# Leftover tokens of a fused attention and SwiGLU kernel: four batches as one seven-product block, with loads, sums and kept results moved

## The chip, the cores and the metric

The kernel runs on one core of one Trainium2 chip. The metric is the device time of one execution in microseconds (us); smaller is better. The profile is one execution recorded by the hardware profiler. In it PE is the matrix engine, PEld its weight loads, DVE the vector engine, ACT the scalar engine, POOL the GpSimd engine and SP the engine that only issues transfers here. SPq, ACTq and POOLq are the instruction queues of those engines where they issue transfers.

## The reference

For each batch and head (8 batches, 8 heads, 576 tokens, 64 per head), `phi` gives weights that squeeze the keys and values into 32 memory rows; the queries attend to these rows; the heads side by side are the input of a gated feed-forward block.

```
a      = softmax(phi, axis=tokens)                 # (b, h, 576, 32)
k_m    = a^T k ;  v_m = a^T v                      # (b, h, 32, 64)
attn   = softmax(q k_m^T / 8)                      # over the 32 rows
x      = heads side by side of attn v_m            # 4608 tokens x 512
g, val = x @ w_gate, x @ w_val                     # 512 x 1536 each
out    = (g * sigmoid(g) * val) @ w_out            # 1536 x 512, float32
```

## The kernel before

The work goes batch by batch. The kernel multiplies `v_m` into the gate and value weights first (`u_round`, L459, giving U), so that x is never formed: gate and value of a batch come straight from the attention weights A (`t_A`) and U. This is done in 24 slots of four matrix products of 288 tokens (`gv_slot`, L544: gate on PE, SiLU on ACT at L531, value on PE, product with the gate on DVE at L537 into `t_h`). The hidden 1536 rows are held as three chunks c of 512. Slots 0 to 7 make chunk 0, 8 to 15 chunk 1, 16 to 23 chunk 2.

The output product of a batch covers 512 of its 576 tokens by Strassen's scheme in Winograd's form (`products`, L676): seven half-size products instead of eight. Each is 12 matrix instructions (three chunks, two row blocks, two token blocks of 128, each 128x256). Sums of the hidden tokens (`t_S`) are made in `chunk_done` (L585): on POOL for chunks 0 and 1, on DVE for chunk 2, four operations of 128x512 each. Weight sums (`t_T`) are made once. The products use three PSUM banks, "s", "a" and "c"; a bank is added to over several products, so a partial result has to be copied aside first (`keep`, L727: p1, q6 and p5 by ACT). DVE adds the kept parts to the banks for c11, c22 and c12 (`add`, L733), and c21 is a copy. The results lie in the tiles o1 and o2 and go out through `store` (L635).

The 64 last tokens of each batch do not fit that scheme. `chunk_done` copies them into `t_x` (L591), which holds a pair of batches, so 128 tokens; `out_rest` (L643) multiplies them in the ordinary way: per pair and half of the columns 12 matrix instructions of 128x256, one copy and two stores. One such half is run in each of the stages of batches 2 to 7, and the last two halves at the end.

The order is written by hand. The loop at L954 runs for batches 2 to 7; one pass is called a stage here. A stage of batch b goes:

- first product of batch b-1, scores of b (`scores`, L396), part of U, and the rest of 36 "units" of b-1's products (a unit is two matrix instructions), among which DVE makes the inverse sums and the normed weights (`z_inv_v`, `norm`), and ACT makes exp(phi) of batch b+1 (`phi_exp`, L174, instruction L176);
- then the 24 slots. Beside slot 8 PE sums keys and values of batch b+1 (`kv_items`, L297), the denominators coming from a tree of sums on POOL (`phi_sum`, L209, tiles `t_es` and `t_ehl`), and at slot 19 to 20 it makes most of U of batch b+1 (`u_three`, L793). The remaining units are laid between the slots (`spread`, L804), some by `take` beside these two.

`spread` gives items fractional slot positions and sorts them. What an engine does is thus the order in which this program emits it; each engine runs its own instructions in that order. POOL also issues the loads of q, phi, k and v (`loads`, L940, four transfers for batch b+2); for b above 2 they are issued at the head of the stage (L984), for b = 2 at slot 7 to 8 (L1021). SP issues stores and the two transposing transfers (`load_qT` L118, `kv_T` L283). At the end, after `box["end"]` is set, stores alternate between SP and ACT (L637).

After the loop come the seven products of batch 7 and the two halves of `out_rest` of the last pair (L1030 to L1038).

Of the kernel before, what the change touches and what calls it, by code (L numbers as in the profile page):

```python
# [14 lines left out]
def kernel(  # L15
# [569 lines left out]
    def chunk_done(b, c):  # L585

        if b % 2 == 0 and c == 0:
            xs[b // 2] = hpool.tile([128, NJF, 2, 64], BF16, tag="xs", name="t_x")

        def ends():  # L590
            nc.gpsimd.tensor_copy(  # L591
                out=xs[b // 2][:, 4 * c:4 * c + 4, b % 2], in_=hts[b, c][:, :, S - 64:S]
            )

        t = upool.tile([128, 4, 2, 256], BF16, tag=f"U{c}" if b == 1 else f"S{c}", name="t_S")
        Ss[b, c] = t
        A11, A12, A21, A22 = blocks(b, c)

        def sums(eng, part=(0, 1, 2, 3)):
            if 0 in part:  # L600
                eng.tensor_tensor(out=t[:, 0], in0=A21, in1=A22, op=ALU.add)  # L601
            terms = ((t[:, 0], A11), (A11, A21), (A12, t[:, 1]))
            for n in part:
                if n:
                    subtract(eng, t[:, n], *terms[n - 1])

        end = c + 1 == NCH
        if (b, c) in ((0, 2), (1, 1), (1, 2)):
            late.append(lambda *part: sums(nc.gpsimd if b else nc.vector, *part))
        else:  # L610
            sums(nc.vector if end else nc.gpsimd)
        if end and b > 1:
            late.append(ends)
        else:
            ends()
        if (b, c) in beside_sums:
            beside_sums[b, c]()

    beside_sums = {
        (0, 0): lambda: (load_phi(3, nc.gpsimd), load_q_group(2, 0)),  # L620
        (1, 0): lambda: (load_q_group(2, 1), load_q(3)),
        (0, 1): lambda: (load_k(3), load_v(3)),
    }

    def token_segments(b, t0, count):
        segs = []
        t = t0
        while t < t0 + count:
            blk, pp = divmod(t, P)
            n = min(P - pp, t0 + count - t)  # L630
            segs.append((t - t0, n, b, 2 * (blk % 3) + blk // 3, pp))
            t += n
        return segs

    def store(t_o, b, t0, count, row=0, cols=slice(0, 512), queues=None):  # L635

        if queues is None and box.get("end"):  # L637
            queues = nc.sync, nc.scalar
        for n, (r0, m, bb, jj, pp) in enumerate(token_segments(b, t0, count)):
            eng = queues[n % len(queues)] if queues else nc.sync  # L640
            eng.dma_start(out=out_r[bb, jj, pp:pp + m, cols], in_=t_o[row + r0:row + r0 + m])

    def out_rest(pair, half):  # L643

        h = DM // 2
        mine = {}
        cols = slice(h * half, h * half + h)

        def unit(n):
            def run():  # L650
                if n == 0:
                    mine["p"] = bank([128, h], FP32, "p_oo")
                for jf in (2 * n, 2 * n + 1):
                    nc.tensor.matmul(  # L654
                        mine["p"],
                        lhsT=xs[pair][:, jf].rearrange("p a t -> p (a t)"),
                        rhs=WO[jf][:, cols],
                        start=(jf == 0),
                        stop=(jf == NJF - 1),
                    )  # L660
                if n == NJF // 2 - 1:
                    t_o = work.tile([128, h], FP32, tag="to", name="t_o")
                    copy("v" if box.get("end") else "a", t_o, mine["p"])
                    done(mine["p"])
                    end = 2 * pair + 2 == B
                    for k in range(2):
                        store(
                            t_o, 2 * pair + k, S - 64, 64, 64 * k, cols,
                            ((nc.sync, nc.scalar)[k],) if end else None,
                        )  # L670

            return run

        return [unit(n) for n in range(NJF // 2)]

    def products(b, by_hand):  # L676

        h = DM // 2
        mine = {}
        lo, hi = slice(0, h), slice(h, DM)  # L680

        def A(e, n):
            return lambda c, m, u: hts[b, c][
                :, 2 * m + e, 256 * n + 128 * u:256 * n + 128 * u + 128
            ]

        def Sx(n):
            return lambda c, m, u: Ss[b, c][:, n, m, 128 * u:128 * u + 128]

        def W_(e, cols):  # L690
# [5 lines left out]
        def product(home, lhs, rhs, after):  # L696
            def unit(k):
                c, m = k // 2, k % 2

                def run():  # L700
                    fresh = k == 0 and home not in mine
                    if fresh:
                        mine[home] = bank([128, 2, h], FP32, f"p_o{home}")
                        mine[home, "new"] = True
                    for u in range(2):
                        nc.tensor.matmul(  # L706
                            mine[home][:, u],
                            lhsT=lhs(c, m, u),
                            rhs=rhs(c, m),
                            start=fresh and u == 0,  # L710
                            stop=(k == 5),
                            skip_group_check=u == 1 or not mine.get((home, "new")),
                        )
                    if k == 5:
                        mine[home, "new"] = False
                        if after in now:
                            now[after]()

                return run

            return [unit(k) for k in range(6)]
# [4 lines left out]

        def keep(name, home):  # L727
            def run():
                nc.scalar.copy(out=tile_of(name, tag=name, bufs=1), in_=mine[home])

            return run

# [3 lines left out]
                done(mine[home])  # L736

        def both(name, t0, cols):
            for u in range(2):
                store(mine[name][:, u, cols], b, t0 + 128 * u, 128, cols=cols)  # L740

        def c11():
            t = tile_of("o1", (128, 2, DM), tag="to")
            add(t[:, :, lo], "a", "p1", True)
            if box.get("end"):
                both("o1", 0, lo)

        def c22():
            t = tile_of("o2", (128, 2, DM), tag="to")
            add(t[:, :, hi], "s", "p5")  # L750
            if box.get("end"):
                both("o2", 256, hi)

        def c12():
            t = mine["o1"]
            add(t[:, :, hi], "c", "q6", True)
            both("o1", 0, hi if box.get("end") else slice(0, DM))

        def c21():
            t = mine["o2"]  # L760
            copy("v" if box.get("end") else "a", t[:, :, lo], mine["s"])
            done(mine["s"])
            both("o2", 256, lo if box.get("end") else slice(0, DM))

        ops = dict(
            p1=keep("p1", "s"), q6=keep("q6", "s"), p5=keep("p5", "c"),
            c11=c11, c22=c22, c12=c12, c21=c21,
        )
        now = {n: f for n, f in ops.items() if n not in by_hand}
        first = product("s", A(0, 0), W_(0, lo), "p1") + product("a", A(1, 0), W_(1, lo), "c11")  # L770
        five = product("c", Sx(0), T(0), "p5")
# [1 line left out]
        three = product("c", Sx(3), W_(1, hi), "c12")  # L773
        seven = product("s", Sx(2), T(2), "c22")
        four = product("s", A(1, 1), T(3), "c21")
        if b + 1 == B:
            return first + six + five + seven + three + four, ops
        return first + five + six + three + seven + four, ops

# [174 lines left out]
    for b in range(2, B):  # L954
# [23 lines left out]
            backlog = one[6:12] + zero[36:] + one[12:36]  # L978
            ops = ops1
        else:  # L980
            backlog += out_rest(b // 2 - 1, b % 2)
            run(take(6))
        if b > 2:
            loads(b)  # L984
        for g in range(NG):
            scores(b, g)
        if b > 2:
# [16 lines left out]
        run(take(12))  # L1004
        if b == 2:
            u_three(2)
            run(out_rest(0, 0))
            u_values(2)
            backlog = one[36:]
        g = gv_slots(b)  # L1010
        beside = 0 if last else min(7, len(backlog))
        outs = [lambda: run(take(1)) for _ in range(len(backlog) - beside)]
        streams = [(g, 0, 24), (outs, 4, 24)]
        if last:
            streams += [([u_item(b, 2)], 5, 6)]
        if not last:
            load_qT(b + 1)
            if b > 2:
                phi_sum(b + 1)
            else:  # L1020
                streams += [([lambda: loads(2)], 7, 8)]  # L1021
            streams += [
                (kv_items(b + 1, lambda: (u_item(b, 2, "aava")(), run(take(2)))), KV, KV + 4),
                ([lambda: (run(take(2)), u_three(b + 1), run(take(3)))], 19, 20),
            ]
        spread(*streams)
        flush_mul()
        units, ops = products(b, ("p1", "c11"))
        backlog += units
    run_late()  # L1030
    run(take(6))
    ops["p1"]()
    run(out_rest(B // 2 - 1, 0))
    box["end"] = True
    run(take(6))
    ops["c11"]()
    run(backlog)
    run(out_rest(B // 2 - 1, 1))  # L1038
# [1 line left out]
_INS = ['q', 'k', 'v', 'phi', 'moe_w_gate', 'moe_w_val', 'moe_w_out']  # L1040
_OUTS = [((4608, 512), 'float32')]
# [25 lines left out]
```

The softmax here doesn't subtract the row's maximum and nothing guards it: scores larger than these inputs give would overflow.

## Time and profile before

| what | value |
|---|---|
| median of 3 runs | 238.11 us (237.35 to 239.08) |
| the profiled execution's own time | 236.3 us |
| its span, first to last instruction | 234.5 us |
| PE busy | 225.9 us (96%) |
| DVE, ACT, POOL busy | 187.4, 172.5, 135.2 us |
| leftover products, L654 | 96 matrix instructions of 128x256 |
| seven-product instructions, L706 | 672 of 128x256 |
| granted clock of PE | 1.000 |
| q, phi, k and v loads, 576 KB each | 7.4, 7.9, 10.1 and 14.4 us median from issue to landing |

Busy time of PE counts an instruction[...], so neighbouring instructions overlap: the mean of 273 ns for a 128x256 instruction isn't what one costs in a row of them. The chain of waits, in which each piece begins where the one before it ends, gives that. The table of busy shares in 40 slices shows in which part of the span an engine works. The table of waits tells for whom an engine stood idle.

### The profile page before, as it was taken

What the parts mean: (1) busy time and instruction counts of PE and PEld (TensorE: products, weight loads), DVE (VectorE), ACT (ScalarE), POOL (GpSimd) and SP (SyncE); (2) the same over time, 40 slices, a digit from 0 to 9 for tenths busy, and PEclk for the clock granted to TensorE, in tenths of its full rate; (3) what the DMA queues carried; (4) which work ended last, traced back from release to release, by engine and by line L of the source; (5) the groups of instructions that cost most, each with busy time, mean ns of one, the idle gap of its engine ahead of it and who ended that gap; (6) DMA issues with size and microseconds to landing.
All of it is one profiled execution on the core that took longest, in us unless ns stands there. A gap on an engine that the chain in (4) does not pass through costs nothing.

```text
span 234.5 us, 7300 instructions
## 1 busy us (share of the span) xinstructions
PE 225.9 (96%) x2847; PEld 171.3 (73%) x2847; DVE 187.4 (80%) x417; ACT 172.5 (74%) x368; POOL 135.2 (58%) x171
## 2 busy tenths in 40 slices
PE   7998899999999999999999999999999999999992
PEld 2555466778887777887778777877788777878881
DVE  4157699999979697998799878988799879987621
ACT  2758888988447888977898779968897789677310
POOL 8532426999099159654992399267916493029400
PEclk9999999999999999999999999999999999999999
DMA  6999999999974999899559964999313721122134
GB/s 211 205 205 207 198 208 206 228 238 248 207 169 97 252 216 158 166 247 232 137 80 252 214 110 106 225 226 142 110 25 81 132 89 27 31 62 89 33 92 126
DMA packets 42914, 36.84 MB, mean 157 GB/s; under 512 B 15488, under 2 KB 38528, under 8 KB 42880
## 3 DMA queue, kind: packets, MB, share of 16 engines
q0 software_dynamic: 21440, 22.42, 55.0%
q1 hardware_dynamic: 20176, 12.79, 25.8%
q10 hardware_dynamic: 1264, 1.18, 1.6%
q8 instruction: 22, 0.36, 0.6%
q14 instruction: 12, 0.10, 0.1%
HBM read 42.47 MB, written 9.44 MB: 221 GB/s over the span
## 4 chain that ended last, share of the span: by engine, by line
PE 82%; DMA 8%; POOL 4%; DVE 3%; issue 1%; ACT 0%; DVEq 0%; POOLq 0%
PE p_g L514 20%; PE p_v L514 19%; PE p_os L706 16%; PE p_oc L706 8%; DMA t_kv<-in_v_dram 8%; PE p_u L471 5%; PE p_oo L654 5%; PE p_oa L706 4%; PE p_kv L235 2%; POOL t_es L217 1%; POOL t_q L108 1%; PE p_g L400 1%; POOL t_kv L98 1%; DVE t_lz L443 1%; DVE t_z L434 1%
## 5 line engine op out<-in xcount | busy, mean ns | idle before, releaser
L537 DVE TENSOR_TENSOR t_h<-t_sg,p_v 128x288 bf16<-128x288 bf16 x192 | 83.1, 452 | 15.6 <-PE p_v L514 7.6
L514 PEld LDWEIGHTS <-t_U 128*128 128x128 bf16 x768 | 73.7, 98 | 21.7 <-issue 2.9
L531 ACT ACTIVATE t_sg<-p_g 128x288 bf16<-128x288 f32 x192 | 74.5, 423 | 15.9 <-PE p_g L514 9.1
L514 PE MATMUL p_g<-t_A,t_U 128*128 128x288 bf16 x384 | 77.2, 286 | 0.0
L514 PE MATMUL p_v<-t_A,t_U 128*128 128x288 bf16 x384 | 77.0, 286 | 0.0
L706 PEld LDWEIGHTS <-t_S 128*128 128x128 bf16 x384 | 37.4, 98 | 4.5 <-issue 0.2
L601 POOL TENSOR_TENSOR t_S<-t_h 128x512 bf16<-128x512 bf16 x17 | 19.7, 1156 | 35.2 <-DVE t_h L537 35.2
L491 ACT CAST t_U<-p_u 128x512 bf16<-128x512 f32 x53 | 28.0, 608 | 8.9 <-PE p_u L471 8.9
L706 PEld LDWEIGHTS <-t_h 128*128 128x128 bf16 x288 | 27.3, 98 | 7.8 <-issue 4.0
L706 PE MATMUL p_os<-t_T,t_S 128*128 128x256 bf16 x192 | 23.7, 273 | 0.0
L559 POOL TENSOR_TENSOR t_S<-t_S,t_h 128x512 bf16<-128x512 bf16 x17 | 19.6, 1155 | 1.3
L559 POOL TENSOR_TENSOR t_S<-t_h,t_S 128x512 bf16<-128x512 bf16 x17 | 20.1, 1186 | 0.0
L559 POOL TENSOR_TENSOR t_S<-t_h 128x512 bf16<-128x512 bf16 x17 | 19.6, 1155 | 0.0
L471 PE MATMUL p_u<-W,t_kT 64*32 64x512 bf16 (+1 forms) x416 | 15.9, 363 | 0.1
L706 PE MATMUL p_os<-t_T,t_h 128*128 128x256 bf16 x96 | 15.6, 273 | 0.0
L827 PE MATMUL p_warm<-bones 128*128 128x512 bf16 (+2 forms) x43 | 12.9, 427 | 1.7 <-DVE bones L850 1.7
L451 DVE TENSOR_TENSOR t_A<-t_E,t_lz 128x576 bf16<-128x576 bf16 x16 | 13.4, 840 | 0.9 <-ACT t_lz L427 0.3
L654 PE MATMUL p_oo<-WO,t_x 128*128 128x256 bf16 x96 | 14.0, 273 | 0.0
L495 DVE CAST t_U<-p_u 128x512 bf16<-128x512 f32 x19 | 12.4, 683 | 1.6 <-PE p_u L471 1.6
L215 POOL COPY t_mark<-t_A 1x1 bf16<-1x1 bf16 x4 | 0.7, 182 | 20.3 <-DVE t_A L451 20.3
L706 PE MATMUL p_oc<-t_T,t_S 128*128 128x256 bf16 x96 | 12.0, 273 | 0.0
L706 PE MATMUL p_oa<-WO,t_h 128*128 128x256 bf16 x96 | 11.8, 273 | 0.0
(93 smaller groups left out, 309.9 us busy)
## 6 DMA issues: line engine op xcount, KB each, us to landing
t_kv<-in_k_dram POOLq DMA_DIRECT2D x8, 576.0 KB, 10.1
t_kv<-in_v_dram POOLq DMA_DIRECT2D x8, 576.0 KB, 14.4
out_dram<-t_o SPq DMA_DIRECT2D x21, 192.0 KB, 2.6
t_phi<-in_phi_dram POOLq DMA_DIRECT2D x6, 576.0 KB, 7.9
t_q<-in_q_dram POOLq DMA_DIRECT2D x5, 576.0 KB, 7.4
out_dram<-t_o SPq DMA_DIRECT2D x37, 64.0 KB, 2.0
out_dram<-t_o SPq DMA_DIRECT2D x14, 128.0 KB, 5.8
t_q<-in_q_dram POOLq DMA_DIRECT2D x6, 288.0 KB, 11.3
```

The lines of the kernel that those rows point to most:

```text
L451: nc.vector.tensor_tensor(out=a, in0=es.pop((b, g)), in1=lzs.pop((b, g)), op=ALU.mult)
L471: nc.tensor.matmul(p[g][32 * i:32 * i + 32, o:o + n], lhsT=kTs[b][64 * g:64 * g + 64, 2, 32 * i:32 * i + 32], rhs=w_part(w, c, i, g, halve ...
L491: nc.scalar.copy(out=t, in_=p)
L495: nc.vector.tensor_copy(out=t, in_=p)
L514: nc.tensor.matmul(p[:, 0:HALF], lhsT=Us[b, c, g][:, o // 2, which, 128 * (o % 2):128 * (o % 2 + 1)], rhs=atts[b, g][:, r], start=(g == 0) ...
L531: nc.scalar.activation(out=sg, in_=gate[:, 0:HALF], func=AF.Silu)
L537: nc.vector.tensor_tensor(out=dst, in0=sg, in1=val[:, 0:HALF], op=ALU.mult)
L559: eng.tensor_tensor(out=out, in0=x, in1=y, op=ALU.subtract)
L601: eng.tensor_tensor(out=t[:, 0], in0=A21, in1=A22, op=ALU.add)
L654: nc.tensor.matmul(mine["p"], lhsT=xs[pair][:, jf].rearrange("p a t -> p (a t)"), rhs=WO[jf][:, cols], start=(jf == 0), stop=(jf == NJF - 1),)
L706: nc.tensor.matmul(mine[home][:, u], lhsT=lhs(c, m, u), rhs=rhs(c, m), start=fresh and u == 0, stop=(k == 5), skip_group_check=u == 1 or n ...
L827: nc.tensor.matmul(p[:, 0:128 * a], lhsT=bones, rhs=x.to_broadcast([128, a, 128]) if a > 1 else bones, start=True, stop=True,)
```

## The change

Four edits:

1. The leftover tokens of four batches (two pairs, 256 tokens) go through the seven-product scheme as well ("quad"), with one token block of 128 instead of two, so 6 matrix instructions to a product. `out_rest` is gone. Quad 0 (batches 0 to 3) is spread over slots 0 to 6 of the stage of batch 4. Of quad 1 (batches 4 to 7) the first two products lie between the slots of the last stage, the other five at the very end. The sums it needs are made by `quad_sums` on POOL, 12 operations of 128x256: for quad 0 in the stage of batch 4, before its scores, and for quad 1 after the last chunk.
2. The loads of batch b+2 are issued in `chunk_done` after the sums of chunk 0, for batch 2 also.
3. The sums of the quads are made in the order in which the products use them, and one term overwrites `t_x`.
4. The results of the quads are put into the second or first half of the tiles p1, q6 and p5 that hold the kept products, and stored from there.

Fewer units are kept back for the `take` calls beside slots 8 and 20 (4 instead of 7), and the stores at the end alternate over a running count.

```diff
             ends()
+        if b > 1 and c == 0:
+            loads(b)
         if (b, c) in beside_sums:
             beside_sums[b, c]()
...
+    def quad_sums(qd):
+        x, y = xs[2 * qd], xs[2 * qd + 1]
...
+        for n in range(4):
+            for c in range(NCH):
+                t = Qs[qd, c]
+                A11, A12, A21, A22 = quarters(c)
+                if n == 0:
+                    nc.gpsimd.tensor_tensor(out=t[:, 0], in0=A21, in1=A22, op=ALU.add)
+                elif n == 1:
+                    subtract(nc.gpsimd, t[:, 1], t[:, 0], A11)
+                elif n == 2:
+                    subtract(nc.gpsimd, A21, A11, A21)
+                else:
+                    subtract(nc.gpsimd, t[:, 2], A12, t[:, 1])
...
-    def out_rest(pair, half):
...
-    def products(b, by_hand):
+    def products(b, by_hand, quad=None):
...
+        U = 2 if quad is None else 1
...
         def keep(name, home):
             def run():
-                nc.scalar.copy(out=tile_of(name, tag=name, bufs=1), in_=mine[home])
+                t = tile_of(name, tag=name, bufs=1)[:, 0:U]
+                mine[name, "all"], mine[name] = mine[name], t
+                nc.scalar.copy(out=t, in_=mine[home])
...
+        def leftover(name, room, half, cols):
+            def run():
+                t = mine[room, "all"][:, half]
...
+        if quad is not None:
+            ops.update(
+                c11=leftover("c11", "p1", 1, lo), c12=leftover("c12", "q6", 1, hi),
+                c22=leftover("c22", "p5", 1, hi), c21=leftover("c21", "q6", 0, lo),
+            )
...
-            backlog += out_rest(b // 2 - 1, b % 2)
             run(take(6))
-        if b > 2:
-            loads(b)
+        if b == 4:
+            run_late()
+            quad_sums(0)
...
-            run(out_rest(0, 0))
+            run(one[36:])
...
-        beside = 0 if last else min(7, len(backlog))
+        quad = []
+        if b == 4:
+            quad = products(b, (), 0)[0]
+        if last:
+            rest, rest_ops = products(b, (), 1)
+            backlog += rest[:12]
+        beside = 0 if last else min(4, len(backlog))
-        streams = [(g, 0, 24), (outs, 4, 24)]
+        streams = [(g, 0, 24), (quad, 0, 6), (outs, 6 if quad else 4, 24)]
...
-                streams += [([lambda: loads(2)], 7, 8)]
...
-                ([lambda: (run(take(2)), u_three(b + 1), run(take(3)))], 19, 20),
+                ([lambda: (u_three(b + 1), run(take(2)))], 19, 20),
...
     run_late()
+    mark = att.tile([1, 1], BF16, tag="mark", bufs=1, name="t_mark")
+    nc.gpsimd.tensor_copy(out=mark, in_=Ss[B - 1, 2][0:1, 3, 0, 0:1])
+    quad_sums(1)
     run(take(6))
     ops["p1"]()
-    run(out_rest(B // 2 - 1, 0))
     box["end"] = True
     run(take(6))
     ops["c11"]()
     run(backlog)
-    run(out_rest(B // 2 - 1, 1))
+    run(rest[12:])
```

## The prediction

> **What bounds the kernel now.** I read the page first: busy shares, and the 40 slices.
>
> ```profile
> PE 225.9 (96%) x2847; PEld 171.3 (73%) x2847; DVE 187.4 (80%) x417; ACT 172.5 (74%) x368; POOL 135.2 (58%) x171
> ...
> PE   7998899999999999999999999999999999999992
> ```
>
> PE is full in every slice from about 30 us to the last one. "Busy" can hide gaps, so the chain of waits is next, here for the end of the span. Its columns are start, duration, engine, tile and line.
>
> ```profile
> 218.37 1.31 PE p_os L706 x12
> 219.68 1.31 PE p_oo L654 x12
> 220.99 1.31 PE p_oa L706 x12
> ...
> 228.85 1.32 PE p_oo L654 x12
> ```
>
> Twelve 128x256 instructions take 1.31 us, whether they belong to a seven-product or to the leftovers: 109 ns each, each piece beginning where the last ended. So PE sets the time, and a PE instruction removed is worth 109 ns where nothing else steps in. One stage, from 118.94 to 144.17 in the chain, is 25.23 us. Its row costs are 96 instructions at 109 ns (10.5), 96 gate and value ones at 122 ns (11.7), scores and first U 0.6, sums of keys and values 0.8, U 1.2: 24.8. Only some 0.4 us of a stage is not PE's own work, about 2 us in five stages.
>
> Then the waits of PE's weight loads (who for whom, us in all, times, longest):
>
> ```profile
> PEld L263 <- POOL t_ehl L224: 0.6, 3, 0.3
> ```
>
> In three of the four stages with this sum (batches 3, 5, 6: 0.32, 0.17 and 0.16 us) PE stands at the denominators until POOL's tree of sums is done. That tree starts when DVE has the normed weights, so here DVE and POOL together already run level with PE.
>
> Last, POOL and ACT in order of time around a stage's turn (batch 3 to batch 4; start, duration, engine, line, instruction):
>
> ```profile
> 109.25 1.15 POOL L601 TENSOR_TENSOR t_S<-t_h 128x512 bf16<-128x512 bf16 x1 [3.25 <-DVE t_h L537]
> ...
> 119.05 0.81 POOL L115 DMA_DIRECT2D t_q<-in_q_dram  x1
> 119.86 0.80 POOL L93 DMA_DIRECT2D t_phi<-in_phi_dram  x1
> ```
>
> ```profile
> 124.08 1.17 ACT L176 ACTIVATE t_ephi<-t_phi 128x1152 bf16<-128x1152 f32 x1
> 125.14 0.58 ACT L729 COPY t_q<-p_os 128x512 f32<-128x512 f32 x1
> ```
>
> The first gives the pace of POOL's sums and the price of issuing loads; the second shows that exp(phi) stands on ACT just ahead of the copy q6 that bank "s" needs before the seventh product.
>
> **What the Trainium skill says.** "TensorE: Matmul & The Clock Gate", section Back-to-back issue gap, gives 262 cycles for 256 columns at 2.4 GHz, 109 ns; the chain agrees (1.31/12). "DMA: Bandwidth & Descriptors", Anatomy of one DMA, says that "any semaphore wait happens on the issuing sequencer before dispatch", so a store issued by ACT that waits for DVE holds up what stands behind it on ACT. At the end of the kernel before, ACT's seven stores fill 4.11 us while it waits for DVE, which fits. "GPSIMD Engine Reference", section 3.1, puts a two-input operation at about 2.6 cycles per element, at 1.2 GHz 1.11 us for 512; the trace has 1.155, so it agrees.
>
> **The change, part by part.**
>
> *PE work.* Out go 8 halves of 12 = 96 instructions; in come 2 quads of 7 x 6 = 84. Minus 12 x 109 ns = **-1.31 us**. Nothing else changes on PE in number. Before the end of the last stage 72 go and 42 + 12 come (-1.96); after it 24 go and 30 come (+0.65).
>
> *Where a filler leaves a wait.* In the order of the changed kernel one unit (two instructions, 0.22 us) that lay between slots 6 and 7 is gone from the stages of batches 3, 5 and 6. It is ahead of the denominators, where PE already waits. The DVE and POOL chain to that point isn't shortened, so the wait grows as much as the work shrinks: 3 x 0.22 = **+0.66**. In batch 4's stage quad 0 stands in front of the denominators (42 x 109 ns = 4.6 us), which hides the rest.
>
> *Sums of the quad on POOL.* No 128x256 bf16 sum is in the trace; bounds are half of 1.155 (0.58) and the float32 row of L217 (0.73). I take 0.60: 12 x 0.60 = 7.2 us. In batch 4's stage POOL then ends: sums of chunk 0 start 8.6 us before the stage's turn (9.69 before the change, less ten instructions), +4.95 with the copy, +3.13 of loads, +4.95 chunk 1, +0.45 copy, +7.2, +4.0 for the tree (127.24 to 131.24 before) = 16.1 us after the turn. PE is at the denominators 12.53 + 4.58 - 0.22 = 16.9 after it. Hidden by 0.8; at 0.73 us a sum it would cost 0.8. Quad 1's sums begin 2.6 us after the last gate product and end at 9.8, before their last use: nothing.
>
> *Loads moved.* Four issues, 0.81 + 0.80 + 0.76 + 0.76 = 3.13 us of POOL, now stand ahead of the sums of chunk 1. Those end about 4.0 us after the turn and are first used 3.75 after it, by the product that needs only the first of them (done at 0.7): nothing. But the data come later against their use. Phi is issued 4.95 + 0.81 = 5.8 us after chunk 0's sums start and lands 7.9 later (four stages: 7.2 to 7.9), so at 13.7. ACT wants it 124.08 - 109.25 = 14.8 less ten instructions (1.09) = 13.7 after the same point. A dead heat. ACT late by d delays q6; q6 ends at 125.72 and the seventh product starts at 126.01 to 126.18, so about 0.3 is free. I take **+0.2** for four stages; bounds 0 and 0.7 each. V, issued at 7.3, lands 13.0 to 13.7 later, at 21 at most, against its use at 20.9; but that row was held up by the transposing transfers, which now run before the loads. Nothing, bounded by 0.5 a stage. The transfer of q into its transposed form, freed of the loads, landed in 6.6 instead of 9.3 to 9.6 us where none ran: no gain, since PE waited 0.2 us for these in all.
>
> *ACT and DVE in the gates.* Each leftover half was one ACT copy (0.41). A quad has three ACT copies, one more copy, three DVE sums (0.42 from the 128x256 row). In quad 0's slots PE has 0.76 us more per slot, which covers them. Elsewhere DVE needs 0.48 us a slot and PE 0.49: fewer fillers take away its catching up. DVE's idle time in those slots was about 2 us, against 1.3 removed: nothing, bounded by 0.4 a stage.
>
> *Result tile p1.* Quad 1's c11 lies in the single buffer p1. Its last product ends 0.73 us before the last gate product, DVE's sum some 0.8 later, SP issues two stores (0.45 each) that land 2.0 after issue: 2.5 us after the turn T. Batch 7's own copy p1, on ACT, needs the buffer and came 1.3 after T. It would end at 3.15, and the third product, which adds to the same bank, is due at 2.62 now that the leftover half no longer lies between. **+0.5** (0.2 to 0.8).
>
> *ACT's queue at the end.* Batch 7's fourth product ends 9.16 after T (84 instructions, without the delay above). DVE's copy takes 0.69 to 9.9, ACT issues two of the four stores, waiting for it: 10.8. Only then comes the quad's q6 copy (0.4), to 11.25. The quad's seventh product, due at 9.16 + 12 x 0.109 = 10.47, adds to that bank: **+0.8** (0.3 to 1.2). Before, an ordinary half lay there, which waits for no copy. The tail (DVE copy 0.42, one store on each queue) is as before.
>
> Sum: -1.31 + 0.66 + 0.2 + 0.5 + 0.8 = **+0.85 us**. The profiled execution would go from a span of 234.5 to 235.4, and from 236.3 to 237.2. The median of the runs lies 1.8 above that execution; the difference is carried over to it: 238.11 + 0.85, **239.0 us**.
>
> **The rivals.**
>
> *The covers hold* (the two waits at the end and the growth at the denominators come to a few tenths): the PE saving remains, 238.11 - 1.31 + 0.3 = 237.1. For it: each wait hangs on differences of under 1 us. Against: buffer p1 and the order on ACT are in the instruction order, and DVE's and POOL's chain isn't shortened.
>
> *Phi comes late* (slower than before). At the turn the loads share the transfer engines with four stores of the batch before. If phi lands 9 us after issue, d is 1.1, PE's seventh product loses 0.8 in each of four stages, +3.2 for 0.2: 242. It decides over the 1% line when phi takes about 8.7 us. Against: at 94.6, with such stores running, it took 7.9. This is also the case in which "a third into the gates" is not what happens: the issue stands behind phi's tree and chunk 0's sums on POOL, nearer the last third.
>
> *DVE becomes the bound in slots without fillers*: 0.4 in batches 3, 5 and 6, +1.2: 240.2. For it: 0.48 against 0.49. Against: DVE's idle 2 us.
>
> **How the numbers follow.** Likeliest case 0.52 (238.3 to 239.8); covers hold 0.22 (236.8 to 238.3); phi late 0.14 (240.3 to 242.5); DVE 0.10 (239.8 to 240.8); something not seen 0.02. A range of 237.1 to 241.0 leaves out the low end of the second and the high half of the third, under 2 in 10. Measurement tells about 1% (2.4 us) from no change. Faster by more than that would need PE's saving and half of all its other time: 0.03. Slower: most of phi late, 0.13. Same: 0.84.
>
> **What would show it.** L654 gone, 84 more at L706's place; the wait at the denominators about 0.4 in batches 3, 5, 6 and none in 4; exp(phi) idle before it, released by its transfer, under 0.5; a gap on PE of about 0.5 before the third product after the last gate, and one of 0.8 before the quad's seventh, with ACT storing. I am wrong if PE's chain has no such gaps (then 237.1), or if ACT waits over 1 us for phi in several stages (then over 241).

## The result and the profile after

| what | before | after |
|---|---|---|
| median of 6 runs | 237.12 us (236.50 to 239.08) | 250.07 us (249.40 to 252.25) |
| ratio | | 1.055, 95% interval 1.049 to 1.061 |
| profiled execution: time, span | 236.3, 234.5 us | 249.44, 247.6 us |

The change makes the kernel 12.9 us slower. The forecast was 239.0 us, with a range of 237.1 to 241.0.

The page of the changed kernel, busy shares and the row of PE in the 40 slices:

```profile
PE 227.4 (92%) x2835; PEld 170.6 (69%) x2835; DVE 198.0 (80%) x423; ACT 172.9 (70%) x368; POOL 154.0 (62%) x196
...
PE   7998999999999999599987999879996999999883
```

PE's 12 instructions are gone (2847 to 2835), as planned, but PE's row, full before, now has holes at slices 17, 21 to 22, 26 to 27 and 31. They are one stage (some 4 to 5 slices of 6.2 us) apart. DVE has 10.6 us more of busy time than before, though only six instructions of 0.42 us have come in.

The table of waits, of PE and of its weight loads (who for whom; us in all, times, longest):

```profile
PE p_g L514 <- DVE t_A L451: 9.6, 4, 2.7
...
PE p_os L715 <- ACT t_q L740: 0.9, 1, 0.9
PE p_os L715 <- ACT t_p L740: 0.8, 1, 0.8
```

```profile
PEld L263 <- POOL t_ehl L224: 1.2, 3, 0.4
```

The first row did not exist before: four times PE stands at the first gate products of a batch, because DVE has not finished the normed weights. The other rows are those that the prediction had: the two gaps of the end, and the denominators (1.2 us, where the kernel before has 0.6).

Where the span grew, in us, measured between the starts of each stage's first product, the "turn" into that stage ("expected" is the kernel before plus what the prediction's steps put into that stage, without the 0.2 for phi):

| part | before | expected | after | after less expected |
|---|---|---|---|---|
| up to the stage of batch 3 | 93.1 | 91.8 | 92.4 | 0.5 |
| stage of batch 3 | 25.6 | 24.5 | 27.5 | 2.9 |
| 4, with quad 0 | 25.2 | 28.5 | 31.4 | 2.9 |
| 5 | 25.3 | 24.2 | 27.0 | 2.7 |
| 6 | 25.3 | 24.2 | 27.0 | 2.8 |
| 7 | 23.6 | 23.6 | 23.8 | 0.2 |
| the end | 16.3 | 18.3 | 18.7 | 0.4 |

So the unexpected loss lies in the stages of batches 3 to 6, 2.7 to 2.9 us in each. PE's four waits for the normed weights are 2.73, 2.40, 2.24 and 2.25 us of it, in this order.

Why DVE is late shows in DVE's own groups. First of the kernel before, then after: the second of the four sums of chunk 2 (us busy in all, mean ns of one, idle before):

```profile
L559 DVE TENSOR_TENSOR t_S<-t_S,t_h 128x512 bf16<-128x512 bf16 x7 | 3.4, 490 | 0.2
```

```profile
L559 DVE TENSOR_TENSOR t_S<-t_S,t_h 128x512 bf16<-128x512 bf16 x7 | 6.5, 934 | 0.2
```

The same instruction, on the same data, takes about twice as long on average; the other three get longer too (442 to 989, 442 to 663 and 462 to 627 ns). What stands beside it is shown by POOL and DVE in order of time at the turn into the stage of batch 4, which is at 119.81 (start, duration, engine, line, instruction):

```profile
118.41 0.75 POOL L102 DMA_DIRECT2D t_kv<-in_v_dram  x1
119.17 1.17 POOL L601 TENSOR_TENSOR t_S<-t_h 128x512 bf16<-128x512 bf16 x1
120.42 1.16 POOL L559 TENSOR_TENSOR t_S<-t_S,t_h 128x512 bf16<-128x512 bf16 x1
121.53 1.34 POOL L559 TENSOR_TENSOR t_S<-t_h 128x512 bf16<-128x512 bf16 x1
122.83 1.33 POOL L559 TENSOR_TENSOR t_S<-t_h,t_S 128x512 bf16<-128x512 bf16 x1
```

```profile
121.13 0.73 DVE L601 TENSOR_TENSOR t_S<-t_h 128x512 bf16<-128x512 bf16 x1
121.89 1.26 DVE L559 TENSOR_TENSOR t_S<-t_S,t_h 128x512 bf16<-128x512 bf16 x1
123.07 1.37 DVE L559 TENSOR_TENSOR t_S<-t_h 128x512 bf16<-128x512 bf16 x1
124.36 0.61 DVE L559 TENSOR_TENSOR t_S<-t_h,t_S 128x512 bf16<-128x512 bf16 x1
...
130.18 1.22 DVE L451 TENSOR_TENSOR t_A<-t_E,t_lz 128x576 bf16<-128x576 bf16 x1
```

The loads end at 119.16, and only then do POOL's sums of chunk 1 begin, 119.17 to 124.16. DVE's sums of chunk 2 fall into the same time. Both engines read two inputs from SBUF, and both get longer. DVE's four sums take 3.77 us from the first start to the start of what follows (121.13 to 124.90), where the kernel before needed 1.65; POOL's last two go from 1.15 to 1.34.

In the kernel before the two rows did not meet. There the turn is at 118.77. POOL's last sum of chunk 1, then DVE's first sum of chunk 2 and the second normed weights:

```profile
117.62 1.16 POOL L559 TENSOR_TENSOR t_S<-t_h,t_S 128x512 bf16<-128x512 bf16 x1
```

```profile
119.65 0.42 DVE L601 TENSOR_TENSOR t_S<-t_h 128x512 bf16<-128x512 bf16 x1
...
126.42 0.76 DVE L451 TENSOR_TENSOR t_A<-t_E,t_lz 128x576 bf16<-128x576 bf16 x1
```

POOL's sums are over at 118.78, and DVE's begin 0.87 us later.

### The profile page after: what moved, and what is told of

Its sections match the earlier page's. It is cut to its first block, busy times and chain, and to the rows that moved or that the text cites. A ratio compares the mean times of both kernels' runs of the same rounds, so it can differ in the third digit from the quotient of the medians.

```text
span 247.6 us, 7309 instructions
## 1 busy us (share of the span) xinstructions
PE 227.4 (92%) x2835; PEld 170.6 (69%) x2835; DVE 198.0 (80%) x423; ACT 172.9 (70%) x368; POOL 154.0 (62%) x196
## 4 chain that ended last, share of the span: by engine, by line
PE 63%; DVE 22%; POOL 4%; issue 4%; ACT 3%; DMA 1%; ACTq 0%; DVEq 0%; SPq 0%; POOLq 0%
PE p_g L514 17%; PE p_v L514 16%; PE p_os L715 11%; DVE t_S L559 5%; PE p_u L471 4%; PE p_warm L862 4%; PE p_oc L715 4%; POOL t_es L217 3%; DVE t_lz L443 3%; DVE t_z L434 3%; DVE t_A L451 2%; DVE t_o L745 2%; DVE t_h L537 2%; PE p_kv L235 2%; PE p_oa L715 2%
## 5 line engine op out<-in xcount | busy, mean ns | idle before, releaser
L537 DVE TENSOR_TENSOR t_h<-t_sg,p_v 128x288 bf16<-128x288 bf16 x192 | 82.0, 452 | 16.9 <-PE p_v L514 5.3
L514 PE MATMUL p_g<-t_A,t_U 128*128 128x288 bf16 x384 | 78.0, 286 | 9.7 <-DVE t_A L451 9.6
L601 POOL TENSOR_TENSOR t_S<-t_h 128x512 bf16<-128x512 bf16 x17 | 19.7, 1160 | 40.3 <-DVE t_h L537 40.2
L559 POOL TENSOR_TENSOR t_S<-t_h,t_S 128x512 bf16<-128x512 bf16 x17 | 20.8, 1228 | 0.0
L559 POOL TENSOR_TENSOR t_S<-t_h 128x512 bf16<-128x512 bf16 x17 | 20.3, 1195 | 0.0
L715 PE MATMUL p_os<-t_T,t_h 128*128 128x256 bf16 x96 | 14.7, 274 | 0.3 <-DVE t_o L745 0.3
L451 DVE TENSOR_TENSOR t_A<-t_E,t_lz 128x576 bf16<-128x576 bf16 x16 | 13.9, 871 | 0.9 <-ACT t_lz L427 0.3
L715 PE MATMUL p_oc<-WO,t_S 128*128 128x256 bf16 x96 | 11.8, 272 | 0.0
L715 PE MATMUL p_os<-WO,t_h 128*128 128x256 bf16 x96 | 11.8, 272 | 0.0
## 6 DMA issues: line engine op xcount, KB each, us to landing
WO<-in_moe_w_out_dram POOLq DMA_DIRECT2D x3, 512.0 KB, 18.7
```

The costliest lines, as they stand in the source:

```text
L451: nc.vector.tensor_tensor(out=a, in0=es.pop((b, g)), in1=lzs.pop((b, g)), op=ALU.mult)
L514: nc.tensor.matmul(p[:, 0:HALF], lhsT=Us[b, c, g][:, o // 2, which, 128 * (o % 2):128 * (o % 2 + 1)], rhs=atts[b, g][:, r], start=(g == 0) ...
L537: nc.vector.tensor_tensor(out=dst, in0=sg, in1=val[:, 0:HALF], op=ALU.mult)
L559: eng.tensor_tensor(out=out, in0=x, in1=y, op=ALU.subtract)
L715: nc.tensor.matmul(mine[home][:, u], lhsT=lhs(c, m, u), rhs=rhs(c, m), start=fresh and u == 0, stop=(k == 5), skip_group_check=u == 1 or n ...
```

## The experiments

Each ratio below is against the kernel before as it was measured beside the run.

The theory: POOL and DVE hinder each other where both run operations with two SBUF inputs. The moved loads cost only because they push POOL's sums of chunk 1 onto DVE's sums of chunk 2. The rivals: the transfers themselves are at fault; or POOL's 12 sums for the quad.

**e1, loads back.** The changed kernel, with the loads where they were before.

```diff
-        if b > 1 and c == 0:
-            loads(b)
...
+        if b > 2:
+            loads(b)
         if b == 4:
             run_late()
             quad_sums(0)
```

> The changed kernel with the loads issued where the kernel before has them (slot 7 to 8 for batch 2, head of the stage for the others), all else as changed. Crowding theory (the moved loads push POOL's sums of chunk 1 into the time of DVE's sums of chunk 2, and the two slow each other down; DVE then is late with the normed weights and PE waits at the first slot): the four DVE sums after batches 2, 3, 5 and so on take 1.3 us again instead of 3.1 to 4.4, PE's waits of 2.2 to 2.7 us at the first slot of batches 3, 5 and 6 vanish, some of batch 4's stays because the quad's sums are on POOL there; time 238 to 241 us. Theory that the quad or its leftovers cause the loss: over 246 us.

Measured: 244.52 to 252.68 us in four runs, too far apart for a ratio. The profile is that of a run of 251.71. In it the waits of PE for the normed weights in batches 3, 5 and 6 are gone, as expected. At the turn into batch 4 there is something new. DVE, and then the first and the last three of POOL's 12 quad sums, in order of time:

```profile
121.49 8.02 DVE L559 TENSOR_TENSOR t_S<-t_h 128x512 bf16<-128x512 bf16 x1
```

```profile
122.30 1.92 POOL L638 TENSOR_TENSOR t_Q<-t_x 128x256 bf16<-128x256 bf16 x3
...
127.94 2.08 POOL L559 TENSOR_TENSOR t_Q<-t_x,t_Q 128x256 bf16<-128x256 bf16 x3
```

One DVE sum of 0.41 us hangs for 8.02, until POOL's row of 12 (122.30 to 130.02) has nearly passed. PE waits 4.12 us for it and 1.30 more for the normed weights. From then on PE's granted clock is at half for some 9 us (a row of twelve matrix instructions takes 2.77 us instead of 1.47). The stage of batch 4 takes 38.0 us instead of 31.4. So quad 0's sums at that place are a hazard of their own; in the changed kernel the late sums of chunk 1 stood between. Two waits for transposing transfers (1.5 and 1.0 us) are new as well. The expected 238 to 241 was missed by every run: with the loads back, the rest of the change still costs at least 8 us. What spreads the four runs was not traced.

**e2, loads only.** The kernel before, with nothing but the loads moved.

```diff
+        if b > 1 and c == 0:
+            loads(b)
         if (b, c) in beside_sums:
...
-        if b > 2:
-            loads(b)
...
-            else:
-                streams += [([lambda: loads(2)], 7, 8)]
```

> The kernel before with nothing changed but the place of the loads (after the sums of chunk 0). Crowding theory: 11 to 12 us slower than before, about 248.5 us, with PE idle 2 to 3 us before the first slot of batches 3, 4, 5 and 6. Theory that the quad causes the loss: within 2 us of before.

Measured: 244.79 us against 236.17, ratio 1.037 (1.033 to 1.040). PE's waits:

```profile
PE p_g L514 <- DVE t_A L451: 7.0, 4, 2.0
```

One edit, for which the prediction had 0.2 us in all and nothing for POOL's sums, costs 8.6 us alone. The size expected was 11 to 12: only the direction was right. Here the leftover instructions of the kernel before are still in place between the slots, and in the stages of batches 4 to 6 DVE is less behind at the turn: its sums begin 0.88 us after it, as before, instead of 1.32. PE waits 7.0 instead of 9.6.

**e3, POOL's time without the transfers.** The kernel before, loads untouched, with eight copies on POOL that nobody reads at the place behind chunk 0's sums. They were planned as 3.1 us and took 3.65.

```diff
+        if 1 < b < 6 and c == 0:
+            for _ in range(8):
+                spare = att.tile([128, 4, 64], BF16, tag="spare", bufs=1, name="t_spare")
+                nc.gpsimd.tensor_copy(out=spare, in_=hts[b, c][:, :, 0:64])
```

> The kernel before with its loads untouched, and eight POOL copies of 128x256 (0.39 us each, 3.1 us in all, their results not used) put where the change issues the loads, for batches 2 to 5. Crowding theory (it is POOL's time that matters, not the data): as slow as with the loads moved, 246 to 249 us, DVE sums of chunk 2 slowed in the same way. Rival (the transfers, running at the turn of the stage, slow DVE or come late): as before, 237 to 238.5 us.

Measured: 245.93 us, ratio 1.041 (1.039 to 1.044).

```profile
PE p_g L514 <- DVE t_A L451: 7.0, 4, 2.5
```

The time is just under the expected 246 to 249. The wait is the same, four times, 7.0 us, though the loads keep their place in the order. In time they are later than before, since POOL comes to them later: in the stage of batch 4 the first is issued at 125.59, when DVE's slow sums (from 122.77) are all but over. In e2 the loads are earlier than before, and the wait is as large. So it is POOL's time that costs, not when the transfers run. Another 1.4 us are three waits for the transposed keys, which e2 does not have.

**e4, POOL's sums held.** The changed kernel; POOL makes the sums of chunk 1 of batches 2 to 5 only after DVE's sums of chunk 2, in order of use.

```diff
+        elif 1 < b < 6 and c == 1:
+            held_sums[b] = sums
...
+        if b in held_sums and end:
+            mark = att.tile([1, 1], BF16, tag="mark", bufs=1, name="t_mark")
+            nc.gpsimd.tensor_copy(out=mark, in_=t[0:1, 3, 0, 0:1])
+            for part in ((0, 1), (3,), (2,)):
+                held_sums[b](nc.gpsimd, part)
```

> The changed kernel, but for batches 2 to 5 POOL's sums of chunk 1 wait until DVE's sums of chunk 2 are done (and come in the order of their use); the loads stay where the change puts them. Crowding theory: DVE's four sums take 1.3 us again, the waits at the first slot shrink from 2.2 to 2.7 us to under 1 (the normed weights, an operation with two inputs, still meets POOL), time 240 to 244 us. Rival (transfers): DVE or PE as late as in the changed kernel, 249 to 251 us, or slower, since the sums come later.

Measured: 244.88 us, ratio 1.038 (1.036 to 1.039), against 1.055 of the changed kernel; 240 to 244 was expected. The row "p_g from t_A" is gone from PE's waits, and DVE's sums are short again:

```profile
L559 DVE TENSOR_TENSOR t_S<-t_S,t_h 128x512 bf16<-128x512 bf16 x7 | 3.1, 447 | 0.2
```

What is taken away here is only that the two rows run at the same time. POOL has the same work, later, and every load stays where the change puts it. The stages of batches 3, 5 and 6 go from 27.0 to 27.5 us down to 25.2 to 25.3, and the span from 247.6 to 243.2: the theory holds, and the rival of the transfers falls for these waits. Left are the stage of batch 4 (32.5 us, more than the 31.4 of the changed kernel, against 28.5 expected), the end, and new waits of PE for POOL's held sums, 0.4 in each stage.

**f1, a row of POOL sums alone.** To see the hang of e1 without the rest of the change: the kernel before, with 12 POOL sums of 128x256 that nobody reads behind the loads in the stage of batch 4. **f2** is the same with a mark that holds the row until DVE's last sum is done.

```diff
+        x, y = (hts[b, 1][:, :, 128 * k:128 * k + 64] for k in range(2))
+        for n in range(12):
+            t = att.tile([128, 4, 64], BF16, tag=f"spare{n % 3}", bufs=1, name="t_spare")
+            nc.gpsimd.tensor_tensor(out=t, in0=x, in1=y, op=ALU.add)
```

> The kernel before, with twelve POOL sums of 128x256 (their results not used, one behind the other without waits) added in the stage of batch 4 right after the loads are issued, where the quad's sums stood in the run with the loads put back. Crowding theory: one of DVE's four sums of chunk 2 hangs until POOL's row of sums is through, 5 to 8 us instead of 0.42, PE waits for it 3 to 6 us in that stage, time 5 to 9 us above before. Rival (the long DVE sum came from the quad's data or its order, not from POOL's work): before's time within 1 us.

> The same twelve POOL sums, but behind a one-element POOL copy that waits for DVE's last sum of chunk 2. Crowding theory: DVE's sums take 0.42 us; only the normed weights (0.76 us before) run 0.2 to 0.6 us longer, and the tree of sums on POOL comes up to 2 us later; time 0 to 3 us above before. Rival (twelve sums cost POOL's time wherever they stand): the same as unheld, 5 us or more.

Measured: f1 243.85 us, ratio 1.030 (1.027 to 1.034); f2 244.17, ratio 1.032 (1.028 to 1.035). The hang came in both, at the next operation of DVE with two SBUF inputs, the normed weights. DVE and POOL in f2:

```profile
122.16 0.78 DVE L443 STREAM_TRANSPOSE t_lz<-t_z 128x576 f32<-128x576 f32 x1
122.97 7.53 DVE L451 TENSOR_TENSOR t_A<-t_E,t_lz 128x576 bf16<-128x576 bf16 x1
```

```profile
122.01 7.54 POOL L624 TENSOR_TENSOR t_spare<-t_h 128x256 bf16<-128x256 bf16 x12
```

DVE's operation with one SBUF input (L443) passes beside the row in its usual 0.78 us. The next one, with two, ends at 130.50, 0.95 us after the row (129.55), for an own time of 0.76. In f1 it takes 5.57 us and ends 0.5 before the row does. f1's time is in the range expected, but the operation that hangs is not one of the four sums. f2 was expected at 0 to 3 us above the kernel before and missed: holding POOL's row behind DVE's sums only moves the hang to the next operation.

The waits are not all of the loss. f1's stage of batch 4 is 8.2 us longer than before; PE waits 5.2 us of that, 2.3 and 2.9 with one instruction between them, and during the second its granted clock falls to half, for some 7 us. In f2 the waits are 3.3 and 2.9, and the half clock lasts some 6 us.

**f3, the quad late.** The changed kernel with the loads as before, quad 0 in the stage of batch 6 with its products spread over slots 0 to 18, and its sums in three groups: behind DVE's last sum, behind the first normed weights, and (half of them) behind POOL's tree; three buffers for `t_x`, two for the results. **f4** is f3 with the end mended: quad 1's p1 in a tile of its own, its q6 and p5 copied by DVE, and the last units of batch 1 behind `u_values(2)`; six buffers instead of eight for the SiLU results make the room.

```diff
-                t = tile_of(name, tag=name, bufs=1)[:, 0:U]
+                t = tile_of(name, tag=name if quad is None or name != "p1" else "Q" + name, bufs=1)[:, 0:U]
...
-                nc.scalar.copy(out=t, in_=mine[home])
+                copy("v" if quad == 1 and name != "p1" else "a", t, mine[home])
```

> The changed kernel with every POOL sum kept off DVE's: the loads where the kernel before issues them; quad 0 in the stage of batch 6, its sums in four groups behind DVE's sums, the first and the second normed weights, and the tree; the leftover tokens of three pairs held at once, two result tiles instead of three, and one unit ahead of slot 8 again. The end is as changed. Crowding theory: no PE wait over 0.5 us in any stage; what is left against before is -1.3 us of PE work and +1.5 to 2 us at the end: 236 to 238 us. If something else in the change costs (fewer fillers, tiles), over 239 us.

> The run before this one with its end mended: quad results c11 in a tile of their own, quad 1's two kept products copied by DVE instead of ACT (behind whose stores they waited), and the last products of batch 1 behind all of batch 2's U. If the two waits at the end are the buffer and ACT's queue: the gaps of 0.8 and 0.9 us at the end go to under 0.2 and the time is 1.4 to 1.9 us below the run before this one, 0 to 1.5 us below before. If they are something else: as the run before this one.

Measured: f3 244.82 us, ratio 1.034 (1.032 to 1.037); f4 242.01, ratio 1.023 (1.020 to 1.026). In neither does PE wait more than 0.2 us for the normed weights. But f3 was expected at 236 to 238, and f4 at or below the kernel before. The new waits of f3 are one for the transposed keys,

```profile
PE p_u L471 <- DMA t_kT<-t_bkv: 2.2, 1, 2.2
```

and one of 0.9 us for the transposed queries. f4 has both too (2.6 and 0.8). With the loads in the old place PE arrives before the keys and queries that SP's transposing transfers bring. In f3 it comes to the keys 1.0 us sooner than before (113.99 instead of 114.98), and their transfer is issued 0.9 later (111.66 instead of 110.76), because the transfer of the queries ahead of it held SP's queue for 7.0 us instead of 6.0. Why that one took longer was not tested. In f4 the two gaps of the end (0.8 and 0.9) are gone, and the end takes 16.6 us instead of 18.7 in f3. The medians differ by 2.8; the 0.7 beyond the end was not traced.

**g1 and g2, the two ways to place the loads.** Both are f4. In g1 POOL issues the loads of batches 3 to 5 behind its tree of phi sums, so about a third into the gates, in its idle time; in g2 they stand where the changed kernel has them and the sums of chunk 1 are held as in e4.

```diff
             if b > 2:
                 phi_sum(b + 1)
+                loads(b)
```

> The kernel of the run f4, with one difference: in the stages of batches 3 to 5 the four loads are issued by POOL behind its tree of phi sums, where it stood idle 3.25 us in the kernel before, so about a third into the gates; for batch 2 they stay at slot 7 to 8. If the waits for the transposed keys and queries in f4 (2.31 and 0.80 us at the third stage's start) come from loads and transposing transfers being on the way together, they go here, and PE finds no wait of its weights either, since POOL's sums of chunk 1 are early again: about 239.0 (238 to 240), 3 us below f4. If they come only from PE being earlier, the wait for kT stays near 2 us: about 242. If phi, issued 11 us later than in f4, comes too late, ACT's exp(phi) waits and PE behind it: 243 or more.

> The kernel of the run f4 with the loads where the changed kernel has them (behind the sums of chunk 0) and with the sums of chunk 1 held until DVE's sums of chunk 2 are done, as in e4. All parts of the change are in, and every crowding found so far is taken away. Theory (crowding of DVE and POOL is the cause, the rest of the loss is the end and the quad's place): the stages come to about 25.2, that of the quad to 29.9, the end to 16.6, so a span near 238.5 and 239.7 (238.5 to 241) against 242.0 of f4. It does not come below the kernel before, since with the sums held the stages are as long as before the change (25.2) though PE has 1.3 us less to do: POOL and DVE then set their length. Rival (transfers are late wherever the loads stand): 242 or more, with a wait of PE for kT as in f4.

Measured: g1 256.78 us, ratio 1.085 (1.082 to 1.088); g2 243.05, ratio 1.026 (1.021 to 1.032). PE's largest wait in g1, and SP's and POOL's queues there in order of time:

```profile
PE p_u L471 <- DMA t_kT<-t_bkv: 13.8, 3, 5.3
```

```profile
107.85 1.23 SPq L289 DMA_TRANSPOSE t_kT<-t_bkv  x1
```

```profile
105.68 0.81 POOL L115 DMA_DIRECT2D t_q<-in_q_dram  x1
...
108.01 0.76 POOL L102 DMA_DIRECT2D t_kv<-in_v_dram  x1
```

The transfer of the keys into their transposed form is issued in the middle of the loads and lands 11.1 us later. Of the cases expected, only the third (243 or more) has room for g1's time, but not for this cause: it has phi late, and here it is the keys. In the changed kernel, where the loads come after it, it takes 3.2. So the place "behind chunk 0's sums" is the one that frees the transposing transfers, and its price is POOL's time. g2 shows the other side: no wait of PE for a transposing transfer is left, the stages of batches 3 to 5 take 25.0 us and the end 16.7, about as expected, but the stage of the quad takes 34.0 instead of 29.9. There POOL, with held sums, six quad sums and then the tree, is late for the denominators (1.0 and 0.3 us of wait, and 0.8 for the scaled keys and values behind them), after which PE runs for 3 us at half its granted clock. One stretch of that stage (its length, then busy us of PE, PEld, DVE, ACT and POOL, PE's granted clock, share and rate of the transfers):

```profile
187.00:190.00 3.00, 3.00 (x14) 1.99 (x14) 1.15 (x2) 1.00 (x2) 1.38 (x3) 0.50 0.16 33
```

So both of g2's expectations fell short: neither the mended kernel's 239.7 nor the rival's late transfers. No version with these parts came below the kernel before.

**g3 and g4, what lets DVE in.** Both are f1, with one run each. g3 puts a small copy (one input) behind each of the 12 sums; in g4 each sum takes the one before it as an input.

```diff
             nc.gpsimd.tensor_tensor(out=t, in0=x, in1=y, op=ALU.add)
+            x = t
```

> The kernel of the run f1 (before, with 12 sums of 128x256 on POOL that nobody reads), with a copy of 128x16, one SBUF input, behind each of the 12. If an operation of DVE with two SBUF inputs hangs because POOL's operations with two SBUF inputs follow each other without a break, it gets in at the first copy: no operation of DVE above 2 us, and the wait of PE at that turn below 1.5 us. If it hangs until POOL has nothing left, or if each of POOL's operations counts whatever its inputs, one DVE operation takes 5 us or more, as in f1 (5.57).

> The kernel of the run f1, in which each of the 12 sums takes the one before it as an input, so that POOL must finish one before it begins the next, as in the sums of a chunk and partly in those of the quads. If the gap between dependent sums is what lets DVE in, no DVE operation takes more than 2 us (sums of 0.7 to 1.4 as in the changed kernel), and POOL's row takes longer than 8 us. If dependence makes no difference, one DVE operation hangs 5 us or more, as in f1.

Measured: g3 244.85 us, g4 241.94 (before 236.52). The normed weights on DVE in g3, then in g4 with POOL's row:

```profile
123.56 7.97 DVE L451 TENSOR_TENSOR t_A<-t_E,t_lz 128x576 bf16<-128x576 bf16 x1
```

```profile
123.12 0.87 DVE L451 TENSOR_TENSOR t_A<-t_E,t_lz 128x576 bf16<-128x576 bf16 x1
...
126.43 0.95 DVE L451 TENSOR_TENSOR t_A<-t_E,t_lz 128x576 bf16<-128x576 bf16 x1
```

```profile
122.71 8.94 POOL L624 TENSOR_TENSOR t_spare<-t_spare,t_h 128x256 bf16<-128x256 bf16 x11
```

Copies between the sums do not help. The chain does: in it POOL's sums take 0.81 us each instead of 0.63, and DVE gets in at once (0.87 and 0.95 for 0.76). Each sum of the chain also reads another tile than in f1, so that it is the gap between dependent sums which lets DVE in is likely, not shown. PE then has no wait for the normed weights, though POOL's tree is late for the denominators (4.1 and 0.3 us), and PE's clock is at half for some 3 us after that. That is what the row costs in g4.

## Why the prediction was wrong

*Failed: "Loads moved."* The step says that POOL's sums of chunk 1 "end about 4.0 us after the turn and are first used 3.75 after it, by the product that needs only the first of them (done at 0.7): nothing". The place was computed rightly (they end 4.35 after the turn, 124.16 less 119.81), and PE did not wait for them. The step put 0.2 us on the moved loads in all; e2 shows 8.6. It asked only who reads the sums' result. It did not ask what else runs in those 4 us. There DVE makes its own four sums, then the normed weights that PE needs next, and the two engines block each other. At the turn into batch 4, the second normed weights end 11.6 us after the turn instead of 8.4: 0.4 because DVE's sums begin later (fewer fillers, see below), 2.1 in the sums themselves, 0.6 in the two normed weights (0.93 and 1.22 for 0.76). PE had about 0.8 us to spare at that point, and stood for the other 2.4. Four such turns are 9.6 of the 12.2 us by which the span forecast (235.4) fell short. e2 and e3 show the cause, e4 its removal.

The Trainium skill names this contention, and the prediction quoted the first of these pages without it: "GPSIMD Engine Reference", section 8, names contention of GpSimd with DVE instructions "with two SBUF inputs", and "SBUF — State Buffer", section SBUF: two separate sides, calls the shared pair of ports an exclusive lock that whoever starts first holds for the whole instruction. The trace of the changed kernel fits: 1.26 us for a sum of 0.42 is its own time and 0.84 of waiting, less than one POOL sum of 1.15. The hang of 8.02 us in e1 and 7.53 in f2 does not fit a lock that is given back after one instruction of 0.63: there a whole row of POOL sums kept DVE out. What the two pages say of a single instruction does not cover this, and the measurement decides.

*Failed in the same way: the sums of the quad.* "Hidden by 0.8" compared POOL's row with PE's arrival at the denominators only. The price per sum was right: 0.60 was taken, 0.64 was measured where POOL runs undisturbed (1.92 for three), 0.73 in batch 4's stage. What was left out is DVE beside it. In the changed kernel the late sums of chunk 1 come first and the row lengthens two normed weights by 0.17 and 0.46; in e1, with the loads back, it costs a hang of 8 us. Why the same row hangs DVE in e1 and not in the changed kernel was not settled. A gap between dependent sums, as in g4, is not the answer: the order of the 12 is the same in both, and in the changed kernel as in e1 most of them take 0.64 to 0.66 us, yet there DVE gets in.

*Held: the PE work.* 12 instructions fewer; the leftover line is gone, and the parts without a new wait (up to batch 3, batch 7) come within 0.5 us of the sum.

*Held: the filler.* The wait at the denominators is 0.41 in batches 3, 5 and 6 and absent in batch 4, as written. The number is in part luck: in e2, where no unit is taken away but PE also stands for the normed weights, the same wait is 0.30 in all four stages. Only some 0.1 of each is the filler's.

*Held: phi.* The row of exp(phi) in the changed kernel:

```profile
L176 ACT ACTIVATE t_ephi<-t_phi 128x1152 bf16<-128x1152 f32 x6 | 7.0, 1166 | 0.2 <-DMA t_phi<-in_phi_dram 0.2
```

0.2 us in one stage: a dead heat indeed. The rival of late phi is excluded. V landed 11.5 to 13.9 us after its issue (13.0 to 13.7 before), so the transposing transfers had hardly held it up; but PE waited for it in none of these stages, as written. The rival of DVE as the bound in slots without fillers is not excluded, and part of it is seen: in the stages of batches 4 to 6 DVE's sums begin 1.32 us after the turn instead of 0.88, and not so in e2, where the fillers are in place. That is 0.4 of three of the waits for the normed weights. Batches 5 and 6 lost some 0.5 us each beyond the wait, and what made that was not traced.

*Held, with the size: the end.* The chain of waits of the changed kernel (start, duration, piece):

```profile
229.69 2.06 DMA out_dram<-t_p
231.84 0.59 ACT t_p L740
232.48 1.47 PE p_os L715 x12
...
240.43 0.45 ACTq L675
240.97 0.38 ACT t_q L740
241.40 0.82 PE p_os L715 x6
```

The store out of the single buffer p1 (2.06 us) holds the copy p1, and PE waits 0.77 (0.5 predicted, 0.2 to 0.8 as bounds). Two stores on ACT stand ahead of the copy q6, and PE waits 0.89 (0.8 predicted). Mended in f4, the end is 2.1 us shorter, somewhat more than the two gaps together. The new order of `u_values(2)` shows no gain: up to the stage of batch 3, f3 and f4 both take 92.5 us.

The likeliest case, and every rival, treated DVE's and POOL's durations as fixed. None of the cases contained the mechanism that decided.

## What to carry to other kernels

When an edit shifts work on POOL, lay DVE's operations with two SBUF inputs beside the new place, not only the readers of POOL's result; a shift of 3 us on an engine with 40% idle time cost 8.6 us here. A PE saving of 1.3 us a stage is worth little where POOL and DVE arrive only 0.8 us ahead of PE: with the crowding taken away, the stages of batches 3 to 5 took 25.0 us (g2), against 25.2 to 25.6 before the change. A place for the loads that frees one transfer may cost another engine its time, so price both before choosing it.

## What the runs showed of the hardware that was not expected

- One DVE operation with two SBUF inputs can be kept out by a row of POOL sums until all or nearly all of the row has passed: 8.02, 5.57, 7.53 and 7.97 us in e1, f1, f2 and g3. It does not always happen: in the changed kernel two such operations took only 0.93 and 1.22 beside a row of 12 sums. DVE operations with one SBUF input were not slowed beside the same rows (0.78 in f2).
- In the one run in which each POOL sum depends on the one before (g4), POOL needs 0.81 us instead of 0.63 for a sum of 128x256, and DVE loses only 0.1 to 0.2 us.
- After a stall of 4.1 us (e1, g4), after two stalls in a row (2.3 and 2.9 us in f1, 3.3 and 2.9 in f2), or after several short ones in 4 us (g2), PE's granted clock was 0.50 for some 3 us (g2, g4), 6 or 7 us (f2, f1) or 9 us (e1). The four single stalls of 2.2 to 2.7 us in the changed kernel were not followed by this: its mean granted clock is 0.997.
- A transposing transfer issued among four loads of 576 KB landed after 11.1 us (g1), and after 3.2 us where the loads are issued later (changed kernel).
